# Packed attention with a gated convolution on one Trainium2 core: the low words of the float64 weights go from DVE to GpSimd, with a new plan and a new issue order

## The chip, the core and the metric

The kernel runs on one core of a Trainium2 chip. The metric is device time in microseconds. A profiled execution gives, beside its own device time, its span: the time from its first to its last instruction. The engines are named as in the profile: PE (TensorE matmul; PEld is its weight load), DVE (VectorE), ACT (ScalarE), POOL (GpSimd) and SP (SyncE, which issues the transfers).

## What is computed

Eight batches of eight heads; 576 positions of 64 values; 32 packed queries per head. Attention is done twice, first from the packed queries to the keys and values, then from the queries to the 32 packed results, and a feed-forward layer follows, in which a convolution of three taps along the sequence makes a gate:

```python
p_packed = sm_attn(p, k, v)                    # [8, 8, 32, 64]
out = sm_attn(q, p_packed, p_packed)           # [8, 8, 576, 64]
x = out.transpose(0, 2, 1, 3).reshape(8, 576, 512)
h = np.maximum(x @ w_in, 0.0)                  # 512 -> 1024
conv_out = sum(conv_w[t] * hp[:, t:t + 576, :] for t in range(3))   # hp: h with a zero at each end
gate = 1.0 / (1.0 + np.exp(-conv_out))
result = h * gate @ w_out                      # 1024 -> 512
```

q, k, v and p are float32. The three weight arrays arrive as float64: the generator multiplies them by a float64 scalar.

## The kernel before

**Groups and tiles.** Four heads of a batch make a group `g` (16 groups, two per batch). `load_kq` and `load_v` bring k, q and v. `head_transpose` turns k and q: groups 0 to 3 with PE (L444) and a copy by ACT (L450), the others with a DVE transpose (L427). `queries` (L484, L487, L493 or L495) prepares the packed queries. `attention` makes the first scores (L460, written `big<-kT,pT`), the maximum on DVE (L515), the exponential on ACT (L519), the product with v (L557), the second scores (L460, `big<-qT,ppT`), a softmax on DVE (L591 to L615) with the exponential on ACT (L601), and splits the weights into a high part (`a2hi`, ACT L619) and a rest (`a2lo`, DVE L621). `packed_weight` multiplies the packed results with half of `w_in` (L641), splits the product in `ghi` (ACT L656) and `glo` (for batches 0 and 1 PE L660 and ACT L664). `ffn1(b, j)` is twelve matmuls of 288 columns (L705) for 128 of the 1024 hidden rows, then ReLU, taps, tanh and gate on ACT and DVE (L717 to L733). `ffn2(m)` multiplies 128 rows of the gated result with `w_out` (L794, split by L744 and L747).

**The float64 weights.** `w_in` and `w_out` come in four tiles each (`load_weight`, L305), 256 rows by 512 columns of 8 bytes, as 128 partitions with 1024 pairs of 32-bit words. They land in three places in turn: `stage`, and two parts of the second gate buffer (`hgt`). `narrow` makes float32 of them in three passes: ACT scales the upper words (L275), DVE turns the low words into a number of 0 to 7 (L277), and DVE puts the two together (L282). The low and the upper pass need only the tile; the third needs both. `conv_w` goes the same way with 24 rows. A tile of `w_out` is then split into `wo_hi` and `wo_lo` with ACT and PE (L333, L338, L342).

**What sets the order.** Every function is a stream of `Step`s, one for each engine instruction or small run of them. The table `ORDER`, two characters a step, says which stream gives the next step; so each engine's queue is written out by hand, and an engine that waits holds all that is behind it. Beside that `Flow` keeps a model of time: when each step could start, with a lag between engines, buffers as tokens and the transfers. Until the first `ffn2` product is done, `Flow.fill` puts `idle` matmuls (L251, 128x128 on the identity matrix) on PE where the model sees PE waiting. The model emits nothing else: it adds no wait to the program. Steps with small stationary tiles (L460, L557, L641) are `tiled`: PE works with 64x32 or 128x32 tiles there.

Of the kernel before, what the change touches and what calls it, by code (L numbers as in the profile page):

```python
# [21 lines left out]
    "0002043m0408043u0304030305060b3l0c06013k050b060c0g0c0c0b060605053q3v3k0e06070e070a3k063v06063k0j060e3v09060j3s0k"  # L22
    "0f0j0o060k0e0f3n0k0i0h3r3r060k0d063k0e0m0d3k3r060d0r0e0e0d060e060e060m060e0m0r3t0m0m3t0s0r400e3w0w0s0e0s0n0z0e0e"
    "3t0s0l0e0n060z0z0l0l0e3y170e46460m0q060m0e0u0e0u0l0m460m0e41460p410m170m0e0m0u17480u3x493x480v410v0m0u3x48410m4a"
    "49484a10474849474a3z0m414948413z491f4a49124248470u0u4a4a474b124b0t490u124b0t14433z0u0t0m4a434b0m4c0t4d1f4b4b434c"
    "0u441f4d0x4c4b3z12120u4e18434e3z1a0u4c120m4d4c4g3o6e130u1a154c3z0u131a124c6e450m0u434e4d45126e0u4e434g4f0m456e4g"
    "1a0u1n0m0u124f6e1n451l4d4e4f6e0u454f4d1a4h1c4e4e0u0u4f4g1b0y1k4d451b4i4f4f114j4i881n884k4i6e1g4h6f4j6e6e4i6f6e4k"
    "4h4k4i4j4i89161i121a4k4j4i6e1i6f6f121e1a4j4k4l891d126f6f6f6f4j4k4l1i6f1o4k6g121s4l1i4l6g4h124l8a4m1a4l6f1a1j4m1q"
    "191j1i1a6f4m4j121i6g1q8a1w6g6h6e4n6g4m6h1q204n1a1v6g1i6g4m1v4l1h6g4m1a4n124m121r1v4n6g6g236f8b1a6g4o121i4n1i4o4p"
    "6h6h4o4p4p1a236h124o8b4o6h4n1q6g4p1a6h6h6h4p6h4o1m4o1a1y4n234p4p1q1i6h1i1q4q282b1y4r6i1r1y6i1y1a1i6i126i6i1q1a2b"  # L30
    "4r6i12241a4q4q1z6i6j1a6i1a4r1i6i6i4s6i2b1p4s6j4s1q4t4u1q4s1i1y1i4t4s264t1t4t1q1z6k1y2g6j2c4u6j1y4u4s261i6j2j4u6j"
    "4s6k6j264u2j4v4t2j1q6j271i4u1u4v226i4u6j266j4t2e1x4w2k6j4t1i4v1q2e1i1q6k4w2e4v2a1i1q6h2f2e4v3p6k6k6k4w1y1i274x26"
    "6k1q6k6l1y4x6l216k6k6k2f4x1q6k4x2m1y4v50266m1q6l6l4w264v1q26262r2m6l2h4w6l2m2r506l4x2r6j6l4y4w2e1q2n2z4y4y2z1y1y"
# [12 lines left out]
    "3i6563613i63633i656162816175747466676587747466757j7h686666676766757575676867836675767575756766686775757j696a7k7k"
    "76697i6868696969766a6a687j6a696876767676766a6a7687766b7g69787h6a7m7k8578876b6b6c7q7676756c6b6c7n6d7o777l7n6c7l7l"
    "6c6d6d6c6d77777i7b777q7m6c7n7n7p6b7m6b6d6b7x6d6d7e817n7o7p7n7n7r79797o777r7777777t7t7o7b777c7e777p7x7s7a7s7c7p7a"
    "7a7a7a7y7a7a7a7u7t7w7w7w7u7a7a7x7v7v7u7z7v7f7f7x7x7y7x7z7x7y7z7d7d7d7d7z7d7d7d7d7y8c7d7d7d7d7d7d7d7d7d8c7d"
# [3 lines left out]
class Step:  # L53
# [5 lines left out]
    def __init__(self, engine, ns, after=(), take=(), give=(), sets=None, cols=0, tiled=False, parts=1, loose=False):  # L59
        self.engine, self.ns, self.after, self.take, self.give = engine, ns, after, take, give  # L60
        self.sets, self.cols, self.tiled, self.parts, self.loose = sets, cols, tiled, parts, loose


class Flow:
# [11 lines left out]
    LAG = {  # L76
        "PE": dict(PE=0, ACT=197, DVE=196, SP=200, POOL=200),
        "ACT": dict(PE=216, ACT=153, DVE=142, SP=200, POOL=200),
        "DVE": dict(PE=256, ACT=128, DVE=127, SP=200, POOL=200),
        "DATA": dict(PE=300, ACT=300, DVE=300, SP=0, POOL=0),  # L80
    }
    ISSUE = dict(SP=(465, 1100), POOL=(1050, 1000))
    LATER, LANES = 620, 8
# [101 lines left out]
def tile_packed_attention_conv_gate(  # L185
# [15 lines left out]
    HG = 4  # L201
# [867 lines left out]
```

## Time and profile before

| | us |
|---|---|
| median of 3 runs (402.21 to 402.48) | 402.41 |
| the profiled execution | 402.01 |
| its span | 400.2 |
| PE busy in the span | 392.2 (98%) |
| DVE busy | 365.5 (91%) |
| ACT busy | 284.1 (71%) |
| POOL busy | 1.6 |

The profile's first part is the busy time of each engine, the second shows it in 40 equal slices. Its table of groups adds up instructions of one line; the timeline lists them in order of time, and writes the idle time of the engine before an instruction in brackets, with what ended it. A line `x14` in a timeline is fourteen records drawn together. A 128x128 float32 matmul of the program leaves two records on PE. PE's ends are modelled and the records overlap, so that what a matmul costs is read from the distance between starts, or between ends.

### The profile page before, as it was taken

How to read it: one execution, taken by the hardware profiler on the slowest of the kernel's cores; microseconds unless marked ns; L12 is line 12 of the kernel's file. 1: busy time of each engine (PE TensorE's matmuls, PEld its weight loads, DVE VectorE, ACT ScalarE, POOL GpSimd, SP SyncE). 2: the span in 40 equal slices, each digit the busy share in tenths (PEclk: the TensorE clock that was granted, in tenths of full speed). 3: DMA queues.
4: the chain of work that ended last, by engine and by line, in shares of the span. 5: the costliest groups of instructions: out<-in, count | busy, mean ns of one | idle time of the engine just before them, and what ended most of it. 6: DMA issues, size and time to landing. Idle time of an engine off the chain costs nothing.

```text
span 400.2 us, 8463 instructions
## 1 busy us (share of the span) xinstructions
PE 392.2 (98%) x3393; PEld 318.8 (80%) x3393; DVE 365.5 (91%) x532; ACT 284.1 (71%) x497; POOL 1.6 (0%) x16
## 2 busy tenths in 40 slices
PE   7899999999999999999999999999999999999996
PEld 6668676778868877878869687878788787889996
DVE  0789999999999999999999999999999999999751
ACT  4989999977687588666765659738657678876440
POOL 1000000000000000000000000000000000000000
PEclk9999999999999999999999999999999999999999
DMA  8999999999858782966483539113600110001202
GB/s 304 357 361 267 276 264 163 128 156 146 121 94 112 122 196 68 156 88 153 79 153 79 97 100 157 48 51 97 122 2 27 52 41 19 23 2 52 78 28 79
DMA packets 140378, 49.19 MB, mean 123 GB/s; under 512 B 121244, under 2 KB 132788, under 8 KB 140340
## 3 DMA queue, kind: packets, MB, share of 16 engines
q1 hardware_dynamic: 140340, 48.67, 55.8%
q8 instruction: 26, 0.43, 0.5%
q14 instruction: 12, 0.10, 0.1%
HBM read 37.25 MB, written 9.44 MB: 117 GB/s over the span
## 4 chain that ended last, share of the span: by engine, by line
PE 84%; ACT 8%; DMA 5%; SPq 1%; issue 1%
PE fo L794 44%; PE big L705 23%; PE big L460 3%; PE big L641 3%; DMA q<-in_q_dram 3%; PE big L926 3%; DMA v<-in_v_dram 2%; PE sm L926 2%; PE sm L557 2%; ACT hgt L731 1%; ACT hgt L721 1%; PE big L547 1%; ACT hgt L275 1%; ACT glo L664 1%; SPq L404 1%; PE sm L794 1%
## 5 line engine op out<-in xcount | busy, mean ns | idle before, releaser
L794 PE MATMUL fo<-wo_hi,xhi 128*128 128x512 f32 x240 | 97.9, 408 | 0.0
L794 PE MATMUL fo<-wo_lo,xhi 128*128 128x512 f32 x240 | 94.8, 395 | 0.0
L794 PE MATMUL fo<-wo_hi,xlo 128*128 128x512 f32 x240 | 94.5, 394 | 0.0
L717 ACT ACTIVATE hbuf<-big 128x576 f32<-128x576 f32 x64 | 42.3, 668 | 30.1 <-PE big L705 29.5
L731 ACT ACTIVATE hgt<-hgt 128x576 f32<-128x576 f32 x64 | 43.9, 696 | 18.8 <-DVE hgt L727 18.6
L794 PEld LDWEIGHTS fo<-wo_hi,xhi 128*128 128x128 f32 x240 | 45.3, 189 | 13.3 <-issue 2.5
L705 PE MATMUL big<-a2hi,ghi 128*128 128x288 f32 x256 | 55.6, 298 | 0.1
L705 PE MATMUL big<-a2hi,glo 128*128 128x288 f32 x256 | 54.5, 294 | 0.0
L705 PE MATMUL big<-a2lo,ghi 128*128 128x288 f32 x256 | 54.3, 294 | 0.0
L794 PEld LDWEIGHTS fo<-wo_lo,xhi 128*128 128x128 f32 x240 | 45.1, 188 | 11.2
L723 DVE SCALAR_TENSOR_TENSOR hgt<-hbuf,cw,hgt 128x576 f32<-128x576 f32 x64 | 51.1, 802 | 2.5 <-ACT hgt L721 2.3
L794 PEld LDWEIGHTS fo<-wo_hi,xlo 128*128 128x128 f32 x240 | 45.1, 188 | 7.9
L727 DVE SCALAR_TENSOR_TENSOR hgt<-hbuf,cw,hgt 128x576 f32<-128x576 f32 x64 | 50.7, 803 | 0.4
L721 ACT ACTIVATE hgt<-hbuf,cw 128x576 f32<-128x576 f32 x64 | 50.3, 792 | 1.0
L733 DVE SCALAR_TENSOR_TENSOR hgt<-hgt,hbuf 128x576 f32<-128x576 f32 x64 | 47.1, 745 | 0.7 <-ACT hgt L731 0.4
L705 PEld LDWEIGHTS big<-a2hi,ghi 128*128 128x128 f32 x256 | 42.7, 188 | 5.1 <-ACT glo L664 1.0
L705 PEld LDWEIGHTS big<-a2lo,ghi 128*128 128x128 f32 x256 | 40.9, 188 | 0.0
L705 PEld LDWEIGHTS big<-a2hi,glo 128*128 128x128 f32 x256 | 40.9, 188 | 0.0
L747 DVE TENSOR_TENSOR xlo<-hgt,xhi 128x1024 fp32r<-128x1024 f32 (+1 forms) x36 | 35.8, 1002 | 0.0
L858 ACT COPY o<-fo 128x512 f32<-128x512 f32 (+1 forms) x32 | 18.5, 580 | 21.2 <-PE fo L794 19.6
L744 ACT CAST xhi<-hgt 128x1024 fp32r<-128x1024 f32 (+1 forms) x36 | 31.5, 881 | 2.2 <-DVE hgt L733 2.2
L515 DVE TENSOR_REDUCE nm<-big 128x1 f32<-128x576 f32 x16 | 11.9, 746 | 11.6 <-PE big L460 11.5
(191 smaller groups left out, 604.1 us busy)
## 6 DMA issues: line engine op xcount, KB each, us to landing
out_dram<-o SPq DMA_DIRECT2D x35, 256.0 KB, 3.3
v<-in_v_dram SPq DMA_DIRECT2D x16, 512.0 KB, 5.9
k<-in_k_dram SPq DMA_DIRECT2D x48, 144.0 KB, 4.2
q<-in_q_dram SPq DMA_DIRECT2D x48, 144.0 KB, 4.1
hgt<-in_moe_w_in_dram SPq DMA_DIRECT2D x3, 1024.0 KB, 11.2
hgt<-in_moe_w_out_dram SPq DMA_DIRECT2D x3, 1024.0 KB, 6.6
a1T<-stage SPq DMA_DIRECT2D x96, 20.0 KB, 1.8
hgt<-in_k_dram SPq DMA_DIRECT2D x2, 576.0 KB, 5.1
```

Source lines behind the costliest of these rows:

```text
L705: nc.tensor.matmul(out=t[:, hf, :SH], lhsT=w[:, gg, js], rhs=x[:, hf * SH : (hf + 1) * SH], start=n == 0, stop=n == 3 * NG - 1,)
L717: nc.scalar.activation(out=h[:, 1 : S + 1].rearrange("c (f s) -> c f s", f=2), in_=t[:, :, :SH], func=AF.Relu, scale=0.5)
L721: nc.scalar.activation(out=d, in_=h[:, 1 : S + 1], func=AF.Copy, scale=cw[:, NJ + j : NJ + j + 1])
L723: nc.vector.scalar_tensor_tensor(out=d, in0=h[:, 0:S], scalar=cw[:, j : j + 1], in1=d, op0=ALU.mult, op1=ALU.add)
L727: nc.vector.scalar_tensor_tensor(out=d, in0=h[:, 2 : S + 2], scalar=cw[:, 2 * NJ + j : 2 * NJ + j + 1], in1=d, op0=ALU.mult, op1=ALU.add)
L731: nc.scalar.activation(out=d, in_=d, func=AF.Tanh)
L733: nc.vector.scalar_tensor_tensor(out=d, in0=d, scalar=1.0, in1=h[:, 1 : S + 1], op0=ALU.add, op1=ALU.mult)
L744: nc.scalar.copy(out=hi[:, js, o], in_=src[:, js])
L747: nc.vector.tensor_tensor(out=lo[:, js, o], in0=src[:, js], in1=hi[:, js, o].bitcast(F32), op=ALU.subtract)
L794: nc.tensor.matmul(out=t[:, : fs.stop - fs.start], lhsT=x, rhs=w[:, c, fs], start=c + i == 0, stop=c == NJ - 1 and i == 2)
L858: nc.scalar.copy(out=o[:, fs], in_=sums_of[m, q][:, : fs.stop - fs.start])
L926: nc.tensor.matmul(out=turns[m, bank][:, at : at + 256], lhsT=x[:, c, :], rhs=y[:, c, :], start=first and c + i == 0, stop=c == 3 and i == ...
```

## The change

The pass over the low words of the eight weight tiles (not that of `conv_w`) is issued on GpSimd in place of DVE. It keeps its operands; the third pass on DVE now waits for GpSimd as well as for ACT. In the model of time, DVE steps that are marked `cols=1` and the GpSimd pass exclude each other (`self.port`): neither starts in the model before the last such step has ended. The GpSimd pass is given 1500 ns there. The model also counts the descriptors of transfers in flight (`ring`), keeps the transfers of SP and GpSimd apart, and has other constants for issue times. `ORDER` is a new table.

```diff
-    ISSUE = dict(SP=(465, 1100), POOL=(1050, 1000))
-    LATER, LANES = 620, 8
+    ISSUE = dict(SP=(465, 1100), POOL=(900, 1000))
+    LATER, LANES = 640, 8
...
+    ROOMY, SLACK = 60000, 500
+    RING = 288
...
+        if step.engine in ("DVE", "POOL") and step.cols:
+            at = max(at, self.port)
         return max(at, self.free[step.engine] + (self.tail(step.tiled) if step.engine == "PE" else 0))
...
                 end = (at + step.ns, engine)
                 self.free[engine] = end[0]
+                if engine != "ACT" and step.cols:
+                    self.port = end[0]
...
+    BY_POOL = range(8)
+    POOL_LOW, POOL_BOTH = 1500, 2200
...
         yield Step("ACT", 93 + m * 14 // 15, after=after, sets=[("up", key)])
         nc.scalar.activation(out=up, in_=up, func=AF.Prelu, scale=F64_REBIAS, alpha=-(2.0**32))
-        yield Step("DVE", 68 + m * 100 // 192, after=after, loose=True)
-        nc.vector.tensor_scalar(
+        pool = key in BY_POOL
+        side = nc.gpsimd if pool else nc.vector
+        at = Step("POOL", POOL_LOW, after=after, loose=True, parts=0, sets=[("low", key)], cols=1)
+        yield at if pool else Step("DVE", 68 + m * 100 // 192, after=after, loose=True, cols=1)
+        side.tensor_scalar(
             out=low.bitcast(I32), in0=low.bitcast(U32), scalar1=2.0**-29, scalar2=7.0, op0=ALU.mult, op1=ALU.min
         )
-        yield Step("DVE", 69 + m * 100 // 96, after=[("up", key)], take=take, sets=sets)
+        yield Step("DVE", 69 + m * 100 // 96, after=[("up", key)] + [("low", key)] * pool, take=take, sets=sets, cols=1)
...
-    "0002043m0408043u0304030305060b3l0c06013k050b060c0g0c0c0b060605053q3v3k0e06070e070a3k063v06063k0j060e3v09060j3s0k"
+    "00040404023m0308050403030505060b0b050c0b0j06060c0c0c0j0j3u06010e0g070706063v3k06063k063q0k060e0e3v0a0k0k0k3v3k3k"
...
```

Ten DVE steps further down (softmax, `a2lo`, taps and gate, `xlo`) get `cols=1` and nothing else. In the changed file a line stands 22 lines further down than before (L444 is L466, L705 is L727), the idle matmul is L270 in place of L251, and the passes of `narrow` are L294, L299 and L304.

The queues show what moved. The first place is PE from the transposes of q of group 2 (`big<-ident,q`) to the first `ffn1` product (`big<-a2hi,ghi`). Before:

```order
L251 MATMUL idle<-ident 128x128 x3
L444 MATMUL big<-ident,q 128x128 x5
L487 MATMUL sm<-ident,pm 128x128
L444 MATMUL big<-ident,q 128x128 x4
L641 MATMUL big<-w_in_sb,ppT 32x512 x8
L557 MATMUL sm<-v,a1T 32x64 x20
L460 MATMUL big<-kT,pT 32x288 x8
L581 MATMUL sm<-ident,pb 128x128
L660 MATMUL big<-ghi,minus 128x512 x2
L460 MATMUL big<-qT,ppT 32x288 x8
L487 MATMUL sm<-ident,pm 128x128
L251 MATMUL idle<-ident 128x128 x7
```

And the same stretch after the change:

```order
L270 MATMUL idle<-ident 128x128
L466 MATMUL big<-ident,q 128x128 x9
L663 MATMUL big<-w_in_sb,ppT 32x512 x8
L579 MATMUL sm<-v,a1T 32x64 x20
L482 MATMUL big<-kT,pT 32x288 x8
L603 MATMUL sm<-ident,pb 128x128
L682 MATMUL big<-ghi,minus 128x512 x2
L270 MATMUL idle<-ident 128x128 x2
L482 MATMUL big<-qT,ppT 32x288 x8
L727 MATMUL big<-a2hi,ghi 128x288 x2
```

The two transposes of packed queries (L487) have gone elsewhere, and seven idle matmuls ahead of the first product have become none, with two ahead of the last scores.

The second is ACT's queue at the same place, up to `glo`, which the first product needs. Before:

```order
L450 COPY qT<-big 128x640
L484 ACTIVATE pm<-p 128x128
L656 CAST ghi<-big 128x1024
L576 ACTIVATE pb<-sm,rs 128x128
L450 COPY qT<-big 128x512
L584 COPY ppT<-sm 128x128
L619 CAST a2hi<-a2t 128x576
L275 ACTIVATE stage<-stage 128x1024
L664 CAST glo<-big 128x1024
```

After:

```order
L472 COPY qT<-big 128x640
L472 COPY qT<-big 128x512
L678 CAST ghi<-big 128x1024
L598 ACTIVATE pb<-sm,rs 128x128
L641 CAST a2hi<-a2t 128x576
L606 COPY ppT<-sm 128x128
L686 CAST glo<-big 128x1024
L294 ACTIVATE stage<-stage 128x1024
```

The upper pass over the fourth tile (`stage`) has gone from ahead of `glo` to behind it.

DVE's queue up to the `a2lo` of group 1, which the first product needs too. Before:

```order
L282 SCALAR_TENSOR_TENSOR w_in_sb<-hgt_77 128x2x512
L604 TENSOR_REDUCE sm_460<-s_425 128x18
L629 RECIPROCAL rs<-rs 128x1
L606 TENSOR_SCALAR sm_460<-sm_460 128x18
L608 RECIPROCAL sm_460<-sm_460 128x18
L621 TENSOR_TENSOR a2lo<-a2t,a2hi 128x576
L610 TENSOR_TENSOR s_425<-s_425,sm_460 128x576
L615 STREAM_TRANSPOSE a2t<-s_425 128x576
L515 TENSOR_REDUCE nm<-big 128x1
L277 TENSOR_SCALAR stage<-stage 128x1024
L591 STREAM_TRANSPOSE s_559<-big 128x576
L621 TENSOR_TENSOR a2lo<-a2t,a2hi 128x576
```

After:

```order
L304 SCALAR_TENSOR_TENSOR w_in_sb<-hgt_77 128x2x512
L626 TENSOR_REDUCE sm_458<-s_404 128x18
L628 TENSOR_SCALAR sm_458<-sm_458 128x18
L630 RECIPROCAL sm_458<-sm_458 128x18
L632 TENSOR_TENSOR s_404<-s_404,sm_458 128x576
L637 STREAM_TRANSPOSE a2t<-s_404 128x576
L537 TENSOR_REDUCE nm<-big 128x1
L643 TENSOR_TENSOR a2lo<-a2t,a2hi 128x576
```

The low pass of `stage` is gone from DVE, and the transpose of group 2's scores now stands behind `a2lo`.

The third place is SP's queue around the q of group 2 (`q<-in_q_dram`). Before:

```order
L305 DMA hgt_77<-in_moe_w_in_dram 128x2x1024
L404 DMA k<-in_k_dram 128x1152
L477 DMA p<-in_p_dram 128x4x64
L404 DMA q<-in_q_dram 128x1152
L388 DMA v<-in_v_dram 128x4x256
```

After:

```order
L327 DMA hgt_77<-in_moe_w_in_dram 128x2x1024
L426 DMA k<-in_k_dram 128x1152
L426 DMA q<-in_q_dram 128x1152
L410 DMA v<-in_v_dram 128x4x256
L414 DMA v<-in_v_dram 64x4x64
```

The second load of packed queries no longer stands ahead of q; it comes four transfers later, and q of group 3 is now issued ahead of the four transfers of k of group 4.

## Rows read from the trace of the kernel before

**Rows 1.** The page: busy time, and the granted clock in 40 slices.
```profile
PE 392.2 (98%) x3393; PEld 318.8 (80%) x3393; DVE 365.5 (91%) x532; ACT 284.1 (71%) x497; POOL 1.6 (0%) x16
...
PEclk9999999999999999999999999999999999999999
```

**Rows 2.** PE's waits: who waited, for whom, us in total, times, longest.
```profile
PE big L444 <- DMA hgt<-in_q_dram: 1.5, 1, 1.5
PE big L444 <- DMA q<-in_q_dram: 0.5, 1, 0.5
...
PE big L444 <- ACT glo L664: 0.2, 1, 0.2
```

**Rows 3.** Windows: length, busy PE PEld DVE ACT POOL, PEclk, DMA share, GB/s.
```profile
20.00:28.00 8.00, 7.57 (x112) 5.48 (x112) 6.87 (x13) 6.12 (x16) 0.00 (x0) 1.00 1.06 358
...
35.00:75.00 40.00, 39.68 (x368) 28.80 (x367) 39.66 (x62) 39.56 (x67) 0.24 (x2) 1.00 1.05 221
```

**Rows 4.** The idle matmuls: durations in ns, first and last start.
```profile
L251 PE MATMUL idle<-ident x70: 271/275/579, 1.7 to 48.3; 128*128 128x128 f32 x70
```

**Rows 5.** PE's timeline, q of group 2 to the first product: start, us, instruction.
```profile
28.18 0.74 PE L444 MATMUL big<-ident,q 128*128 128x128 f32 x5 [0.54 <-DMA q<-in_q_dram]
...
32.64 0.71 PE L460 MATMUL big<-qT,ppT 64*32 64x288 f32 x16
...
33.45 1.73 PE L251 MATMUL idle<-ident 128*128 128x128 f32 x14
34.93 0.51 PE L705 MATMUL big<-a2hi,ghi 128*128 128x288 f32 x2
```

**Rows 6.** ACT's timeline ahead of the first product.
```profile
32.45 0.68 ACT L619 CAST a2hi<-a2t 128x576 fp32r<-128x576 f32 x1
33.03 1.17 ACT L275 ACTIVATE stage<-stage 128x1024 f32<-128x1024 f32 x1
34.07 1.02 ACT L664 CAST glo<-big 128x1024 fp32r<-128x1024 f32 x1
```

**Rows 7.** DVE's timeline ahead of the first product, and at one later low pass.
```profile
32.61 0.69 DVE L277 TENSOR_SCALAR stage<-stage 128x1024 int32<-128x1024 uint32 x1
...
34.17 0.71 DVE L621 TENSOR_TENSOR a2lo<-a2t,a2hi 128x576 fp32r<-128x576 f32 x1
...
63.92 0.69 DVE L277 TENSOR_SCALAR hgt<-hgt 128x1024 int32<-128x1024 uint32 x1
64.53 0.17 DVE L606 TENSOR_SCALAR sm<-sm 128x18 f32<-128x18 f32 x1
```

**Rows 8.** Three groups of POOL: busy us, mean ns of one, idle before.
```profile
L246 POOL MEMSET v<- 64x256 f32 x2 | 0.6, 306 | 0.0
masks.py:199 POOL TENSOR_SCALAR_AFFINE_SELECT ident<-ident 128x128 f32<-128x128 f32 x1 | 0.3, 287 | 0.0
...
masks.py:197 POOL MEMSET ident<- 128x128 f32 x1 | 0.2, 205 | 0.3 <-POOLq L1054 0.3
```

**Rows 9.** Timeline: the first `xlo` and the product that uses it.
```profile
61.27 0.68 DVE L747 TENSOR_TENSOR xlo<-hgt,xhi 128x512 fp32r<-128x512 f32 x1
...
63.54 0.48 PE L794 MATMUL fo<-wo_hi,xhi 128*128 128x512 f32 x1
```

**Rows 10.** PE's timeline around three tiled steps in a row.
```profile
80.28 0.63 PE L660 MATMUL big<-ghi,minus 128*128 128x512 f32 x2
80.84 0.72 PE L460 MATMUL big<-kT,pT 64*32 64x288 f32 x16
81.35 0.69 PE L460 MATMUL big<-qT,ppT 64*32 64x288 f32 x16
81.97 0.77 PE L557 MATMUL sm<-v,a1T 128*32 128x64 f32 x40
82.67 0.50 PE L794 MATMUL fo<-wo_hi,xhi 128*128 128x512 f32 x1
83.01 0.39 PE L794 MATMUL fo<-wo_hi,xlo 128*128 128x512 f32 x1
```

More of the change, by code (lines that the diff above doesn't have):

```diff
@@ L50, with __init__ @@
+    "7b7a7z7a7a777u7w7y7c7a7x7s7s7v7v7a7x7z7a7x7v7y7y7a7e7x7y7a7d7d7d7d7a7d7d7d7z7z7a7d8c8c7d7d7d7d7d7d7d7d7d7d"
 )
 class Step:
-    def __init__(self, engine, ns, after=(), take=(), give=(), sets=None, cols=0, tiled=False, parts=1, loose=False):
+    def __init__(self, engine, ns, after=(), take=(), give=(), sets=None, cols=0, tiled=False, parts=1, loose=False, ring=8):
         self.engine, self.ns, self.after, self.take, self.give = engine, ns, after, take, give
-        self.sets, self.cols, self.tiled, self.parts, self.loose = sets, cols, tiled, parts, loose
+        self.sets, self.cols, self.tiled, self.parts, self.loose, self.ring = sets, cols, tiled, parts, loose, ring
@@ L90, in __init__ @@
         self.free = dict(PE=2500.0, ACT=1900.0, DVE=600.0, SP=580.0, POOL=1350.0)
-        self.data = 2700.0
+        self.data = dict(SP=2700.0, POOL=2700.0)
         self.issued = 0
         self.flights = [0.0] * 7
+        self.queued = []
+        self.port = 0.0
         self.windows = {}
@@ L147, in transfers @@
                 at = max(at, self.flights.pop(0))
+                while self.queued and (self.queued[0][0] <= at or sum(n for _, n in self.queued) + step.ring > self.RING):
+                    at = max(at, self.queued.pop(0)[0])
             at += self.LATER if step.engine == "SP" and self.issued >= self.LANES else issue
             self.issued += step.engine == "SP"
-            slow = next((x for t, x in self.SLOW if self.data < t), 1.0)
-            self.data = max(self.data, at + delay) + step.ns / step.parts * slow
+            slow = next((x for t, x in self.SLOW if self.data["SP"] < t), 1.0)
+            ns = step.ns / step.parts * slow
+            start = max(self.data[step.engine], at + delay)
             if step.engine == "SP":
-                self.flights.append(self.data)
-        return at, self.data
+                landed = self.data["SP"] = start + ns
+                self.flights.append(landed)
+                self.queued.append((landed, step.ring))
+            else:
+                landed = self.data["POOL"] = start + min(max(0.0, self.data["SP"] - start), ns) + ns
+                self.data["SP"] = max(self.data["SP"], start) + ns
+        return at, landed + (self.SLACK if at > self.ROOMY else 0.0)
     def run(self, order):
@@ L169, in run @@
                 self.tiled = step.tiled
-            elif step.engine in self.ISSUE:
+            elif step.engine in self.ISSUE and step.parts:
                 self.free[engine], t = self.transfers(step, at)
@@ L301, in load_weight @@
         _, _, src, st = weight_tile(i)
-        yield Step("SP", 2500, after=[("wp", i - 3)] if i >= 3 else [], sets=[("wd", i)])
+        yield Step("SP", 2500, after=[("wp", i - 3)] if i >= 3 else [], sets=[("wd", i)], ring=16)
         if src.dtype != F32:
@@ L384, in load_v @@
         b, gg = divmod(g, NG)
-        yield Step("SP", 2250, take=["v"], sets=[("v", g)], parts=2)
+        yield Step("SP", 2250, take=["v"], sets=[("v", g)], parts=2, ring=24)
         t = grp[g]["v"] = vfree.pop(0)
@@ L725, in ffn1 @@
         )
[L726 removed]
+        yield Step("DVE", 729, cols=1)
         nc.vector.scalar_tensor_tensor(
@@ L744, in convert @@
             nc.scalar.copy(out=hi[:, js, o], in_=src[:, js])
-        yield Step("DVE", 68 + (js.stop - js.start) * 128 * 100 // 96, sets=spans)
+        yield Step("DVE", 68 + (js.stop - js.start) * 128 * 100 // 96, sets=spans, cols=1)
         for src, o in cuts:
@@ L850, in load_block @@
             nc.scalar.copy(out=hi[:, :, o], in_=src[:, js])
-        yield Step("DVE", 601, sets=[("x", m, k)])
+        yield Step("DVE", 601, sets=[("x", m, k)], cols=1)
         for src, o in cuts_of(m):
```

69 lines of the change are left out of this document (34 added, 35 removed).

## The prediction

> **What bounds the kernel now.** First the busy times: PE is busy for 392.2 us of a span of 400.2, DVE for 365.5, ACT for 284.1, and POOL for 1.6 [rows 1]. So PE sets the end, and the question is where its time is not work. Next PE's waits: the largest behind the start are for two transfers of q, 1.5 and 0.5 us, and the smallest is 0.2 for `glo` [rows 2]; all belong to the first groups and batches. The windows say the same: from 35 to 75 us PE is busy for 39.68 of 40 us, and so are DVE (39.66) and ACT (39.56) [rows 3]. The list of waits has no entry for a later stage. There is one more kind of lost time that is not called idle: the idle matmuls, 70 records, 35 instructions, all between 1.7 and 48.3 us [rows 4]. Fourteen records stand between 33.45 and 34.93 us [rows 5], so one costs 1.48 / 14 = 0.106 us and all of them 7.4 us.
>
> A gain can therefore come only from three places on PE: fewer idle matmuls, shorter waits in the first 50 us, and cheaper changes between tiled and plain matmuls. All other matmuls are the same before and after the change, in number and in shape.
>
> **The change part by part.** *DVE loses eight passes.* One lasts 0.69 us, and the next instruction starts 0.61 us after it (63.92 to 64.53) [rows 7]: 8 x 0.61 = 4.9 us less for DVE. That is not yet a gain, since DVE is not what ends last.
>
> *GpSimd gets eight passes.* No row shows one. Two memsets bound it from below: 205 ns for 128 elements a partition and 306 for 256 [rows 8], so 0.8 ns an element and 0.1 us fixed, 0.9 us for 1024. From above, the select on 128 elements, 287 ns [rows 8], taken eight times: 2.3 us. I take the select, which reads and computes as the new pass does, with the fixed 0.1 us counted once: 1.47 ns an element, 1.6 us. On the path I cost it at nothing: a pass needs only its tile, GpSimd has nothing else to do then, and the third pass also waits for ACT's pass over the upper words, 1.17 us [rows 6], which stands in a busy queue. If that cover is gone, as for the first tile that lands, 1.6 - 1.17 = 0.4 us (at most 1.1) are late on a DVE that still has gaps.
>
> *The third pass gets a wait.* Behind it in DVE's queue stand the softmax of a group and its `a2lo`; PE waits for these. With GpSimd starting at the landing, the wait ends before ACT's.
>
> *Two engines at one port.* The changed plan holds apart the GpSimd pass and DVE steps with two operands in SBUF. It emits no wait for it; if the chip lets only one of them run, DVE stands still for what is left of a pass. The trace of before has no such pair. The bounds are 0 and 8 x 1.6 = 12.8 us of DVE's time; below zero there is nothing, as neither engine gets faster by the other's work. Ahead of the first product about half of DVE's instructions read two SBUF operands, so I take half of a pass, 6.4 us. Against the 4.9 saved DVE is then 1.5 us later by 64 us. The first `xlo` ends at 61.27 + 0.68 = 61.95 and is used at 63.54 [rows 9]: 1.6 us of cover, which this just fills. Cost on PE: 0.
>
> *The order up to the first `ffn1` product.* In before it starts at 34.93 us [rows 5], behind three things, and all three move.
> - PE. q of group 2 was released by its transfer at 28.18. The 128 KB of packed queries ahead of it go away: 0.128 MB at 358 GB/s [rows 3] is 0.36 us, so 27.8. From there to the last scores it took 32.64 - 28.18 = 4.46 us [rows 5]; less one plain transpose of packed queries (0.1), plus four idle records (0.4): 4.8. With 0.65 for the scores themselves [rows 10] the queue can reach the product at 27.8 + 4.8 + 0.65 = 33.3.
> - ACT. `glo` started at 34.07, behind `stage`'s upper pass, which held ACT from 33.03 to 34.07 [rows 6]. That pass is now behind it, and the chain starts 0.36 earlier: `glo` is written near 33.7. The product started 0.16 before the end of `glo`'s record (34.07 + 1.02 = 35.09), so here near 33.5.
> - DVE. `a2lo` started at 34.17, behind a low pass at 32.61 and a transpose of scores; its `a2hi` had ended at 32.45 + 0.68 = 33.13 [rows 6, 7]. With both out of the way it starts when `a2hi` is there, near 32.8, and ends near 33.5.
> The last of the three gives 33.5: 34.9 - 33.5 = 1.4 us earlier. The 1.5 us that went into fourteen idle records are gone with it; they are the same gain and are not counted twice.
>
> *Behind it.* The idle matmuls there were four, and are eight: 4 x 2 x 0.106 = 0.85 us lost, if the waits that they fill are real. What stays of the gain is 1.4 - 0.85 = 0.55.
>
> *Tiled runs.* Scores directly behind other scores end 0.48 us after them, behind plain matmuls 0.65 (80.28 + 0.63 = 80.91, then 81.56, then 82.04); the first plain product behind tiled work ends 0.43 us after it, the next 0.23 [rows 10]. So entering costs 0.16 and leaving 0.20. The 63 tiled steps stand in 30 runs before and 28 after. Counted through both queues, two products with `w_in` save an entry, one score loses one, and two exits are saved: -0.32 + 0.16 - 0.40 = -0.55 us, the most of it behind 75 us where nothing hides it.
>
> *Moved transfers and the rest.* q of group 3 goes ahead of the four transfers of k of group 4: 0.576 MB, some 1.6 us later at 358 GB/s. DVE's transpose of that k has moved by more, behind six gate instructions in place of one, so nothing. The load of packed queries that comes later feeds group 4, which is not needed ahead of 33 us. The model's new constants emit nothing but idle matmuls, which are counted.
>
> *Sum.* 0.55 + 0.55 = 1.1 us. A second way of counting goes through PE's whole queue and leaves the waits as they are: 4 idle instructions less, 0.85, and the runs, 0.55: 1.4. I take the middle, 1.25 us. The profiled execution lasted 402.01 us and would last 400.8; the median of the runs is 0.4 above it, 402.41, and gives 401.2.
>
> **The rivals.** *The gain is given back.* ACT gets nothing off its queue, and has 0.4 us to spare in the 40 us behind the first product [rows 3]. An earlier product only makes PE wait for ACT's copies and ReLUs there; what is left is the tiled runs, partly: 402.1 (401.6 to 403.2). For it: three engines are full at once. Against it: ACT's own pass in front of `glo` is what moved, so ACT's later work moves with PE's.
>
> *The port.* Here the two engines exclude each other on the chip, and a pass meets a two-operand instruction nearly always. In the stretch behind 39 us DVE's queue is mostly gate instructions, and each has two operands in SBUF. Six of eight passes cost DVE their whole 1.6 us: 9.6 - 4.9 = 4.7 us late. Less the cover of 1.6, PE loses 3.1 and keeps the 1.25: 402.4 + 1.9 = 404.3. It decides from a loss of some 1 us a pass (8 x 1 = 4.9 + 1.6 + 1.25, about), or from passes of over 2 us. For it: nothing in the program keeps the two apart, only the order. The Trainium skill has this as a rule (SBUF — State Buffer, "Who interferes with whom"): the port pair that GpSimd shares with DVE is a lock that the first one holds for its whole instruction, also against a DVE instruction with two SBUF inputs if GpSimd reads SBUF. By that rule this rival's mechanism is real and only the meetings are open; no row of before shows it. Against it: the new order has one-operand instructions at several of the landings.
>
> *The clock.* The granted clock is full in all slices [rows 1]. Ahead of the first product there are 23 idle instructions in place of 31, and PE's wait for q of group 1 has fewer of them in front. If the clock falls to 1.2 GHz for a stretch of 4 us there, some 3 us of matmuls last 3 us more, less what the next transfer hides: 404. Against it: the wait is no longer than before.
>
> *The passes stay a cost without a benefit*, that is, DVE's relief is real but PE never waited for DVE: this is the case in the first rival, with the same time.
>
> **How the numbers follow.** The forecast, 399.9 to 401.6, has 0.54: the unknown terms are the waits behind the first product (-0.85 to +0.5) and the DVE cover. A larger gain, below 399.9, has 0.04: it needs PE's waits in 35 to 75 us to go as well. The gain given back, 0.20. The port, 0.16, and the clock, 0.06. A measurement of this kernel can tell some 0.2% from no change, 0.8 us, that is 401.6 to 403.2. Faster: 0.54 + 0.04 = 0.58. Same: 0.20. Slower: 0.22. The range from 399.9 to 403.6 holds the forecast, the gain given back and the mild end of the port, 0.8 in all.
>
> **What would show it.** In the profile of after: 62 records of idle matmuls; the first `ffn1` product at 33.5 us and q of group 2 released at 27.8; `glo` ahead of the upper pass on ACT; GpSimd passes of 0.9 to 2.3 us. For the port: DVE instructions with two operands that last longer than 0.7 to 0.8 us, or idle time in front of them, while GpSimd is busy. The prediction is wrong if the first product is early and PE then waits for ACT or DVE between 35 and 75 us, if DVE's gate instructions are stretched, or if the clock shows less than 9 in a slice behind the first.

## The result and the profile after

| | before | after |
|---|---|---|
| median, us | 402.45 (402.21 to 403.31) | 405.87 (405.35 to 406.36) |
| profiled execution, us | 402.01 | 405.85 |
| its span, us | 400.2 | 404.1 |
| last matmul ends, us | 397.10 | 399.94 |

The changed kernel is slower: the ratio of the times is 1.0080, with a 95% interval from 1.0062 to 1.0098, some 3.2 us. The forecast was 401.2, in a range up to 403.6. Medians here and below are of fast executions alone: one of 571.58 us (e4, whose median with it is 402.58) and one of 767.73 (e10) are left out. Line numbers after are 22 higher than before; for the idle matmuls and the passes over the weights 19 to 22.

The page first, as in [rows 1]: busy time, and the granted clock in 40 slices.

```profile
PE 393.5 (97%) x3385; PEld 319.2 (79%) x3385; DVE 365.2 (90%) x524; ACT 284.0 (70%) x497; POOL 34.2 (8%) x24
PEclk9999999999999999999999999999999999999999
```

Two things stand there. The clock was full throughout. And GpSimd was busy for 34.2 us in place of 1.6: eight passes, so about 4 us each, where the forecast took 1.6 and bounded it at 2.3. DVE has eight instructions fewer and is only 0.3 us less busy.

Six of the eight passes in GpSimd's timeline (start, duration, instruction, and in brackets the idle time in front with what ended it):

```profile
10.90 3.82 POOL L299 TENSOR_SCALAR stage<-stage 128x1024 int32<-128x1024 uint32 x1 [8.95 <-DMA stage<-in_moe_w_in_dram]
24.56 4.09 POOL L299 TENSOR_SCALAR hgt<-hgt 128x1024 int32<-128x1024 uint32 x1 [3.57 <-DMA hgt<-in_moe_w_in_dram]
32.27 3.79 POOL L299 TENSOR_SCALAR stage<-stage 128x1024 int32<-128x1024 uint32 x1 [3.62 <-DMA stage<-in_moe_w_out_dram]
36.14 3.86 POOL L299 TENSOR_SCALAR hgt<-hgt 128x1024 int32<-128x1024 uint32 x1
43.81 3.99 POOL L299 TENSOR_SCALAR hgt<-hgt 128x1024 int32<-128x1024 uint32 x1 [3.81 <-DMA hgt<-in_moe_w_out_dram]
49.16 4.72 POOL L299 TENSOR_SCALAR hgt<-hgt 128x1024 int32<-128x1024 uint32 x1 [1.36 <-DVE hgt L749]
```

And the third passes in DVE's timeline, the first, third, fourth and fifth of eight:

```profile
14.76 1.23 DVE L304 SCALAR_TENSOR_TENSOR w_in_sb<-stage 128x1024 int32<-128x1024 int32 x1 [1.02 <-POOL stage L299]
28.69 1.23 DVE L304 SCALAR_TENSOR_TENSOR w_in_sb<-hgt 128x1024 int32<-128x1024 int32 x1 [1.39 <-POOL hgt L299]
36.34 2.02 DVE L304 SCALAR_TENSOR_TENSOR tmp<-stage 128x1024 int32<-128x1024 int32 x1
40.03 1.25 DVE L304 SCALAR_TENSOR_TENSOR w_in_sb<-hgt 128x1024 int32<-128x1024 int32 x1 [1.68 <-ACT hgt L743]
```

DVE waits 1.02, 1.39 and 1.68 us in front of three of them, 4.1 us in all. The third wait is put down to ACT, but the pass over that tile ran from 36.14 to 40.00 and DVE went on at 40.03: it was GpSimd again. That pass also started late, because the pass of 32.27 held GpSimd until 36.06. The instruction at 36.34 shows the other thing: it met the start of a GpSimd pass at 36.14 and lasted 2.02 us, where others of its line last 1.18 to 1.25.

On PE, where [rows 2] had 0.2 us of waiting for ACT in all, there is now a list. These are PE's waits for ACT of 0.4 us and more (us in total, times, longest):

```profile
PE big L727 <- ACT a L541: 0.7, 1, 0.7
PE big L727 <- ACT glo L686: 0.5, 2, 0.3
PE sm L603 <- ACT pb L598: 0.4, 1, 0.4
PE big L482 <- ACT hbuf L739: 0.4, 1, 0.4
```

They stand in this part of PE's timeline. The first row is the products with `w_in`, the second the first `ffn1` product, whose start was forecast:

```profile
28.85 2.19 PE L663 MATMUL big<-w_in_sb,ppT 64*32 64x512 f32 x16
34.54 0.52 PE L727 MATMUL big<-a2hi,ghi 128*128 128x288 f32 x2 [0.20 <-ACT glo L686]
49.18 0.72 PE L482 MATMUL big<-kT,pT 64*32 64x288 f32 x16 [0.36 <-ACT hbuf L739]
53.10 0.33 PE L603 MATMUL sm<-ident,pb 128*128 128x128 f32 x1 [0.44 <-ACT pb L598]
54.16 0.53 PE L727 MATMUL big<-a2hi,ghi 128*128 128x288 f32 x2 [0.73 <-ACT a L541]
```

The sixteen products with `w_in` (L663) took 2.19 us. They need the tile whose third pass ended at 28.69 + 1.23 = 29.92, after a GpSimd pass that ended at 28.65. The waiting is inside the row, between its eighth and ninth matmul, and the list of PE's waits doesn't name it. Only the rows of this line alone do: PE's weight load sat idle for 1.0 us until DVE's third pass (L304). Behind 57 us PE waits for nothing, as before. The delay has been collected by then and is carried to the end.

### The profile page after: what moved, and what is told of

Same layout as the page of the kernel before. It is cut to its first block, busy times and chain, and to the rows that moved or that the text cites. A ratio compares the mean times of both kernels' runs of the same rounds, so it can differ in the third digit from the quotient of the medians.

```text
span 404.1 us, 8464 instructions
## 1 busy us (share of the span) xinstructions
PE 393.5 (97%) x3385; PEld 319.2 (79%) x3385; DVE 365.2 (90%) x524; ACT 284.0 (70%) x497; POOL 34.2 (8%) x24
## 4 chain that ended last, share of the span: by engine, by line
PE 86%; DMA 5%; DVE 3%; ACT 3%; POOL 1%; SPq 1%; issue 0%; DVEq 0%; ACTq 0%
PE fo L816 44%; PE big L727 23%; PE big L482 3%; PE big L663 3%; DMA hgt<-in_moe_w_in_dram 3%; PE big L948 3%; DMA v<-in_v_dram 2%; PE sm L948 2%; PE sm L579 2%; PE big L360 2%; POOL hgt L299 1%; PE big L569 1%; PE sm L816 1%; DVE w_in_sb L304 1%; DVE hgt L755 1%; ACT hgt L294 1%
## 5 line engine op out<-in xcount | busy, mean ns | idle before, releaser
L816 PE MATMUL fo<-wo_hi,xhi 128*128 128x512 f32 (+1 forms) x244 | 98.9, 405 | 0.0
L816 PE MATMUL fo<-wo_lo,xhi 128*128 128x512 f32 (+1 forms) x244 | 95.9, 393 | 0.0
L816 PE MATMUL fo<-wo_hi,xlo 128*128 128x512 f32 (+1 forms) x244 | 95.7, 392 | 0.0
L816 PEld LDWEIGHTS fo<-wo_hi,xhi 128*128 128x128 f32 x244 | 46.0, 189 | 14.7 <-issue 2.2
L727 PE MATMUL big<-a2hi,ghi 128*128 128x288 f32 x256 | 55.5, 298 | 1.2 <-ACT a L541 0.7
L745 DVE SCALAR_TENSOR_TENSOR hgt<-hbuf,cw,hgt 128x576 f32<-128x576 f32 x64 | 52.1, 820 | 3.2 <-ACT hgt L743 3.0
L816 PEld LDWEIGHTS fo<-wo_lo,xhi 128*128 128x128 f32 x244 | 45.8, 188 | 11.1
L727 PE MATMUL big<-a2hi,glo 128*128 128x288 f32 x256 | 54.4, 294 | 0.0
L727 PE MATMUL big<-a2lo,ghi 128*128 128x288 f32 x256 | 54.2, 293 | 0.0
L816 PEld LDWEIGHTS fo<-wo_hi,xlo 128*128 128x128 f32 x244 | 45.9, 188 | 8.2
L749 DVE SCALAR_TENSOR_TENSOR hgt<-hbuf,cw,hgt 128x576 f32<-128x576 f32 x64 | 51.8, 820 | 0.5
L743 ACT ACTIVATE hgt<-hbuf,cw 128x576 f32<-128x576 f32 x64 | 49.2, 778 | 0.9
L727 PEld LDWEIGHTS big<-a2hi,ghi 128*128 128x128 f32 x256 | 42.5, 188 | 7.3 <-ACT glo L686 1.6
L727 PEld LDWEIGHTS big<-a2lo,ghi 128*128 128x128 f32 x256 | 40.9, 188 | 0.0
L727 PEld LDWEIGHTS big<-a2hi,glo 128*128 128x128 f32 x256 | 40.9, 188 | 0.0
L299 POOL TENSOR_SCALAR hgt<-hgt 128x1024 int32<-128x1024 uint32 x6 | 25.0, 4160 | 19.5 <-DMA hgt<-in_moe_w_out_dram 12.1
```

What stands on the lines that cost most here:

```text
L299: side.tensor_scalar(out=low.bitcast(I32), in0=low.bitcast(U32), scalar1=2.0**-29, scalar2=7.0, op0=ALU.mult, op1=ALU.min)
L727: nc.tensor.matmul(out=t[:, hf, :SH], lhsT=w[:, gg, js], rhs=x[:, hf * SH : (hf + 1) * SH], start=n == 0, stop=n == 3 * NG - 1,)
L743: nc.scalar.activation(out=d, in_=h[:, 1 : S + 1], func=AF.Copy, scale=cw[:, NJ + j : NJ + j + 1])
L745: nc.vector.scalar_tensor_tensor(out=d, in0=h[:, 0:S], scalar=cw[:, j : j + 1], in1=d, op0=ALU.mult, op1=ALU.add)
L749: nc.vector.scalar_tensor_tensor(out=d, in0=h[:, 2 : S + 2], scalar=cw[:, 2 * NJ + j : 2 * NJ + j + 1], in1=d, op0=ALU.mult, op1=ALU.add)
L816: nc.tensor.matmul(out=t[:, : fs.stop - fs.start], lhsT=x, rhs=w[:, c, fs], start=c + i == 0, stop=c == NJ - 1 and i == 2)
```

## The experiments

Three causes were held against each other: the **length** of GpSimd's pass (the third pass waits for it), the **port** (DVE's instructions with two operands in SBUF are held up while GpSimd works), and the **order** (the new issue order is worse, whichever engine makes the passes). All ratios are to the kernel before, timed on the same chip; 0.001 is 0.4 us.

| run | what it is | median us | ratio, 95% interval |
|---|---|---|---|
| after | the changed kernel | 405.87 | 1.0080 (1.0062 to 1.0098) |
| e1 | new order, passes on DVE | 401.36 | 0.9970 (0.9955 to 0.9986) |
| e2 | old order, passes on GpSimd | 405.90 | 1.0077 (1.0050 to 1.0104) |
| e2z | e2, third pass doesn't wait | 403.01 | 1.0007 (0.9993 to 1.0021) |
| e8 | after, third pass doesn't wait | 402.06 | 1.0000 (0.9978 to 1.0021) |
| e4b | after, pass over one pair | 401.76 | 0.9974 (0.9962 to 0.9987) |
| e4 | after, pass over half of the pairs | 402.27 | 0.9998 (0.9980 to 1.0017) |
| e5 | after, pass of one operation | 403.83 | 1.0024 (1.0010 to 1.0039) |
| e3 | after, only `w_out` on GpSimd | 405.28 | 1.0074 (1.0048 to 1.0100) |
| e10 | after, one store cut in eight | 405.09 | 1.0063 (1.0040 to 1.0086) |
| e8s | e8, one store cut in eight | 401.17 | 0.9966 (0.9946 to 0.9987) |
| e4bs | e4b, one store cut in eight | 400.89 | 0.9955 (0.9939 to 0.9972) |

### The engine against the order: e1 and e2

```diff
-        side = nc.gpsimd if pool else nc.vector      # e1, in the changed kernel
+        side = nc.vector
...
-        nc.vector.tensor_scalar(                     # e2, in the kernel before
+        side = nc.gpsimd if key in range(8) else nc.vector
+        side.tensor_scalar(
```

> The changed kernel with its order, its plan and its 31 idle instructions, only that all eight low passes run on DVE again, at the places where the plan lets them start. The three causes that stand against each other: the length of a GpSimd pass (3.8 to 4.7 us in the profile of after, so that DVE's third pass waits for it, 1.0 us at 14.8, 1.4 at 28.7, 1.7 at 40.0); the port (DVE instructions with two operands in SBUF lasted 0.8 to 0.9 us longer where a pass begins, some 3.7 us over the kernel); the new order itself, whichever engine makes the pass. By length or port the loss goes with GpSimd's passes: 401.2 to 403.0, near or under the kernel before, with DVE 4.9 us busier. By the order the time stays at 405 or more, since DVE then has its eight passes on top.

> The kernel before, with its order, its plan and its 35 idle instructions, only that the eight low passes run on GpSimd. By length or port it becomes slower by about what the changed kernel lost, 404.5 to 408: the third passes stand at 14.6, 18.9, 27.4, 36.1 and 38.0 us there, each 2 to 4 us behind the landing of its tile, so those with under 3.8 us wait. By the order alone it gains what DVE is relieved of, or nothing: 401 to 402.6.

e1 is 1.2 us faster than the kernel before, and e2 is 3.1 us slower. So the order isn't the cause: the loss comes and goes with the engine that makes the pass, under either order. e1 is also a version that beats both kernels.

The same two places in e1's trace, PE's products with `w_in` and first `ffn1` product:

```profile
29.14 1.09 PE L663 MATMUL big<-w_in_sb,ppT 64*32 64x512 f32 x16
33.65 0.53 PE L727 MATMUL big<-a2hi,ghi 128*128 128x288 f32 x2
```

and three of DVE's third passes, which now wait for nothing:

```profile
27.81 1.23 DVE L304 SCALAR_TENSOR_TENSOR w_in_sb<-hgt 128x1024 int32<-128x1024 int32 x1
37.38 1.22 DVE L304 SCALAR_TENSOR_TENSOR w_in_sb<-hgt 128x1024 int32<-128x1024 int32 x1
46.33 1.22 DVE L304 SCALAR_TENSOR_TENSOR tmp<-hgt 128x1024 int32<-128x1024 int32 x1
```

The sixteen products take 1.09 us in place of 2.19, and the first `ffn1` product starts at 33.65: the forecast had said 33.5.

Since e1 and after issue the same matmuls in the same order, the delay can be read place by place, as the start of one instruction in both timelines (us):

| place | e1 | after | later |
|---|---|---|---|
| first `ffn1` product (L727) | 33.65 | 34.54 | 0.9 |
| first scores from keys behind 47 us (L482) | 47.62 | 49.18 | 1.6 |
| transpose of packed results (L603) | 50.55 | 53.10 | 2.6 |
| first `ffn2` product (L816) | 65.07 | 68.17 | 3.1 |
| end of the last matmul | 396.74 | 399.94 | 3.2 |

### The wait against the port: e8 and e2z

```diff
+        if pool:
+            low = hbuf[0][:, 0:1].broadcast_to([128, m])   # a column of zeros
...
         nc.vector.scalar_tensor_tensor(
             out=out,
...
```

> The changed kernel, with GpSimd's passes as they are, but the third pass of these eight tiles takes a column of zeros in place of the low words, so it doesn't wait for GpSimd any more (left out: the three lowest bits of the weights). What is left of GpSimd's passes is their use of the port. If their length is the cause, the waits in front of the third pass fall to under 0.3 us and the time to 401.5 to 403.0, although the two-operand instructions on DVE are still stretched by 0.8 us. If it is the port, the stretched instructions and the time stay, 404.5 to 406. If it is the order, both are wrong and the time stays too.

> The order of the kernel before, the eight passes on GpSimd, and zeros in place of the low words for the third pass, so that it doesn't wait (left out: the three lowest bits of the weights). With the wait this order took 405.9. If the waits for a pass of 3.8 us are the cause there too, it falls to 402 to 402.6, the time of the kernel before; if the port is, it stays above 404.5.

GpSimd's passes are all there, as long as before (3.8 to 4.2 us in e8), and the loss is gone: from 1.0080 to 1.0000 under the new order, from 1.0077 to 1.0007 under the old. That is the wait, 3.2 and 2.8 us. In e2's trace six third passes wait for GpSimd, 6.0 us in all, and in the traces of e8 and e2z none does. (e2z's median is 0.4 us over its expected range; the kernel before, timed beside it, was 0.3 over its usual 402.4.) The instruction that met the start of a pass was still stretched, as the fourth third pass of e8 shows:

```profile
36.66 2.04 DVE L309 SCALAR_TENSOR_TENSOR tmp<-stage,hbuf 128x1024 int32<-128x1024 int32 x1
```

So the port is real, but by the medians it isn't what the kernel lost by. It isn't free in every execution. The profiled ones lasted 404.74 us (e8) and 403.48 (e8s, the same with one store cut, see below), where the medians are 402.06 and 401.17. In that of e8s no third pass waits for GpSimd and the clock is full, and yet the last matmul ends at 398.58, 2.4 us later than in its partner with a pass of 0.2 us (e4bs, 396.13). DVE's rows are stretched by some 5 us in sum there, and two of the stretched ones stand in front of the places where PE is late in after, too:

```profile
24.97 1.70 DVE L648 TENSOR_TENSOR a2lo<-a2t,a2hi 128x576 fp32r<-128x576 f32 x1
48.62 2.35 DVE L760 SCALAR_TENSOR_TENSOR hgt<-hgt,hbuf 128x576 f32<-128x576 f32 x2
```

In e4bs the first lasts 0.75 us. In e8s the first tile also landed 1.2 us later (12.05 us, in e4bs 10.88), so not all of the 2.4 need be the port's. What sets such an execution apart from the median one no run shows.

### How long may the pass be: e4b, e4 and e5

```diff
+        part = low[:, : 1] if pool else low           # e4b; in e4: low[:, : m // 2]
...
-            out=low.bitcast(I32), in0=low.bitcast(U32), scalar1=2.0**-29, scalar2=7.0, op0=ALU.mult, op1=ALU.min
+            out=part.bitcast(I32), in0=part.bitcast(U32), scalar1=2.0**-29, scalar2=7.0, op0=ALU.mult, op1=ALU.min
...
+            side.tensor_scalar(out=low.bitcast(I32), in0=low.bitcast(U32), scalar1=2.0**-29, scalar2=None, op0=ALU.mult)   # e5, all pairs
```

> The changed kernel, with a low pass on GpSimd over one pair a partition in place of 1024, whose result the third pass reads for all weights (left out: the low words of all other pairs). So the wait's place, the engine and the order stay, and the pass is some 0.1 to 0.3 us long. By length or port 401.0 to 402.5, the time that was forecast for a pass that costs nothing on the path; what lies between this run and the one with zeros for low words is the price of the port alone. By the order it stays at 405 to 406.

> The changed kernel with GpSimd's pass over 512 pairs a partition in place of 1024; the third pass takes each low word for two weights (left out: the low words of the other half of the pairs). The pass should last half of 3.8 us, 1.9, which is inside the bounds that the prediction set for it (0.9 to 2.3). If the mis-sized pass is all that was wrong, the waits in front of the third pass are gone at this length and the time is 401.2 to 402.3. If the loss grows in proportion to the pass, whatever it covers, half of it stays, 403.4 to 404.

> The changed kernel with a GpSimd pass of one operation, the multiplication, without the minimum (changed: the largest low words give 8 in place of 7). In the measurement alone that pass lasted 2.85 us in place of 3.72. A point between the pass of 2.0 us (402.6) and that of 3.8 (405.9). By the length theory each third pass that waited 1.0 to 1.7 us waits 0.9 less: 403 to 404.2.

| pass, us (most of the eight) | DVE's waits for it, sum, us | ratio |
|---|---|---|
| 0.2 (e4b) | 0 | 0.9974 |
| 2.0 (e4) | 1.1 | 0.9998 |
| 3.0 (e5) | 2.5 | 1.0024 |
| 3.9 (after) | 4.1 | 1.0080 |

The time follows the pass. e4's time, 402.27, lies at the upper edge of what was expected, but the waits, expected to be gone, are not: 0.31 and 0.78 us remain. By the ratios it is 1.0 us slower than e4b, just clear of the noise; in the traces its last matmul ends 0.5 us later (396.71 and 396.22). So a pass of 2.0 us is cheap, but not shown to be free. The third pass of the second `w_out` tile still waits, and so does that of e5. The rows of GpSimd and DVE for this tile, first e4, then e5:

```profile
44.68 2.01 POOL L300 TENSOR_SCALAR hgt<-hgt 128x512 int32<-128x512 uint32 x1 [7.36 <-DMA hgt<-in_moe_w_out_dram]
46.73 1.23 DVE L309 SCALAR_TENSOR_TENSOR tmp<-hgt 128x1024 int32<-128x1024 int32 x1 [0.78 <-POOL hgt L300]
```

```profile
43.79 3.31 POOL L300 TENSOR_SCALAR hgt<-hgt 128x1024 int32<-128x1024 uint32 x1 [5.74 <-DMA hgt<-in_moe_w_out_dram]
47.14 1.23 DVE L307 SCALAR_TENSOR_TENSOR tmp<-hgt 128x1024 int32<-128x1024 int32 x1 [0.86 <-POOL hgt L300]
```

GpSimd starts as the tile lands, at 44.68 and 43.79; DVE's queue is there at 46.73 - 0.78 = 45.95 and 47.14 - 0.86 = 46.28. So there are 1.3 and 2.5 us for the pass, and what it takes beyond that is a wait.

### Which tiles: e3

```diff
-        side = nc.gpsimd if pool else nc.vector
+        side = nc.gpsimd if pool and key >= 4 else nc.vector
```

> The changed kernel, with only the four w_out tiles left to GpSimd; the four w_in tiles have their low pass on DVE. All three waits for GpSimd that the profile of after shows stand at w_in tiles, and the four longest stretches of DVE instructions with two operands in SBUF (36.3, 43.3, 50.2 and 62.8 us) at the w_out tiles. If the wait for a long pass is the cause, the time falls to 401.2 to 402.6. If the port is, it keeps most of the loss: 404 to 405.5.

405.28: by the number the port was right, but the trace shows a wait as well. The expectation of the length theory had looked only at the waits that after shows. Without those at the `w_in` tiles, DVE's queue comes earlier to the second `w_out` tile, and a wait stands there that after had hidden behind the earlier ones. DVE's timeline in e3:

```profile
48.05 1.23 DVE L304 SCALAR_TENSOR_TENSOR tmp<-hgt 128x1024 int32<-128x1024 int32 x1 [1.77 <-POOL hgt L299]
49.20 2.35 DVE L755 SCALAR_TENSOR_TENSOR hgt<-hgt,hbuf 128x576 f32<-128x576 f32 x2
51.54 0.73 DVE L537 TENSOR_REDUCE nm<-big 128x1 f32<-128x576 f32 x1
```

Behind the wait of 1.77 us come two gate instructions, stretched from 1.43 (e1) to 2.35 by the start of the next pass, and behind them the maximum that ACT's exponential needs, for which PE waits. Up to there PE is within 0.6 us of e1; the transpose of packed results starts 1.6 us later (52.13), the first `ffn2` product 2.1 (67.19). Wait and stretch together are 2.7 us here, so this run alone doesn't separate the two causes; e8 does by its median, since all stretches and no waits are in it. Another 0.8 us of e3's distance to e1 comes behind the last matmul (3.94 us to the end, in place of 3.17; see e10).

### The pass and the port by themselves: m1

No diff: a program of its own, which does nothing of the computation.

> No part of the computation: a measurement of the pass and of the port alone. GpSimd makes the pass in several forms (as it is; multiplication only; int32 to int32; float32 to float32; contiguous; in halves), beside a row of DVE instructions with two operands in SBUF, with one, and with one of two in PSUM, and with DVE idle. By the length theory the pass lasts 3.8 us alone too, so it isn't contention that makes it long. By the port theory DVE's instructions with two operands in SBUF stop for the whole pass, 3.8 us, or their sum grows by at least that; by what the profile of after shows only one of them, the one that the pass's start meets, grows by 0.8 to 1.2 us. Those with one operand, or with one in PSUM, keep their time.

GpSimd's pass alone, with DVE idle: as it is, with multiplication only, and over contiguous words.

```profile
84.50 3.72 POOL L53 TENSOR_SCALAR words<-words 128x1024 int32<-128x1024 uint32 x1
88.98 2.85 POOL L53 TENSOR_SCALAR words<-words 128x1024 int32<-128x1024 uint32 x1
101.55 3.63 POOL L53 TENSOR_SCALAR flat<-flat 128x1024 int32<-128x1024 uint32 x1
```

Now DVE's row: two operands in SBUF beside one pass, without a pass; then one operand, in the same two ways; then one of two operands in PSUM, beside a pass (ns: least, median, most).

```profile
L58 DVE TENSOR_TENSOR z<-x,y x10: 748/758/1517, 10.3 to 18.2; 128x576 f32<-128x576 f32 x10
L58 DVE TENSOR_TENSOR z<-x,y x4: 748/758/759, 7.0 to 9.4; 128x576 f32<-128x576 f32 x4
L61 DVE TENSOR_SCALAR z<-x x10: 450/460/1221, 30.0 to 36.0; 128x576 f32<-128x576 f32 x10
L61 DVE TENSOR_SCALAR z<-x x4: 449/460/461, 27.9 to 29.4; 128x576 f32<-128x576 f32 x4
L64 DVE TENSOR_TENSOR z<-bank,y x10: 680/691/691, 46.1 to 52.6; 128x512 f32<-128x512 f32 x10
```

The length theory holds: 3.72 us with nothing beside it. The second operation costs 0.87 of it, the stride of two words 0.09; int32 or float32 in place of uint32 changed nothing. The port theory holds in part. One of the ten instructions with two operands grew by 0.76 us, to 1.52; the others keep their 0.76 although the pass goes on. It is not the one that runs as the pass begins at 11.23 us (11.12 to 11.88) but the next, from 11.91; and the pass is longer beside it, 4.27 us. Against the expectation the instructions with one operand in SBUF are held up too, two of ten, by 0.76 each. The one with an operand in PSUM is not.

### The last microsecond: e10, e8s and e4bs

```diff
-        nc.sync.dma_start(out=...[m * 128 : (m + 1) * 128, fs], in_=o[:, fs])
+        r = 16 if m == 27 else 128
+        for h in range(0, 128, r):
+            nc.sync.dma_start(out=...[m * 128 + h : m * 128 + h + r, fs], in_=o[h : h + r, fs])
```

> The changed kernel, with the store of one earlier block of 128 output rows cut into eight of 16 rows, which only makes SyncE's program seven issues longer. In the trace of after one packet of 8 KB of queue 14, the queue of instructions, lies at 401.45 us, between the issue and the landing of the last stored half block, and from the last matmul to the end it takes 4.13 us; in the kernel before, and with the passes on DVE, the packet comes after the landing and it takes 3.13 and 3.17. If that fetch belongs to SyncE's program and delays the landing, its place moves and the time falls by 1.0 us, to 404.9. If the last microsecond has another cause, the time stays at 405.9.

> Zeros in place of the low words, so that no third pass waits for GpSimd, and the earlier store cut into eight, so that the fetch of code is out of the last landing. What is left of GpSimd's passes is the port: beside a pass of 3.8 us one DVE instruction in the measurement alone grew by 0.76 us, 8 x 0.76 = 6.1 us of DVE's time for the 4.9 that it was relieved of. If PE's end follows DVE there, this run is 0.5 to 1.2 us above its partner with the short pass; if the cover takes it, both agree within 0.4. Without the 0.9 of the fetch: 400.9 to 401.6.

> The partner: GpSimd's pass over one pair a partition, with the same store cut into eight. No wait, no port, no fetch in the last landing: the new order with DVE relieved of eight passes. 400.6 to 401.2, 0.9 under the same kernel without the cut store (401.76); the difference to the new order with the passes on DVE (401.36) is then all that the relief of DVE is worth, 0.2 to 0.7 us.

The last two stores, of half a block each, in the list of transfers (count, KB, median us from issue to landing): first after, then e1, then e10.

```profile
out_dram<-o SPq DMA_DIRECT2D x2, 128.0 KB, 2.7
```

```profile
out_dram<-o SPq DMA_DIRECT2D x2, 128.0 KB, 1.7
```

```profile
out_dram<-o SPq DMA_DIRECT2D x8, 32.0 KB, 1.7
out_dram<-o SPq DMA_DIRECT2D x2, 128.0 KB, 1.7
```

With the longer program on SyncE the packet of the instruction queue moves from 401.45 to 397.82 us, the landing takes 1.7 us again, and the time from the last matmul to the end falls from 4.13 to 3.10 us. In the medians it is 0.7 us (1.0080 to 1.0063), in the pair e4b and e4bs 0.8. The intervals overlap; the microsecond itself is in the traces. It isn't peculiar to after: in six of the thirteen traces (after, e3, e4, e4b, e5, e8) the packet lies between the issue and the landing of the last store, and from the last matmul to the end it takes 3.75 to 4.13 us; in the seven others it doesn't, and it takes 3.10 to 3.17. The table of passes above has it in all four rows.

e8s and e4bs differ by the port alone: 0.9966 and 0.9955, 0.4 us, which the intervals don't tell from nothing. The same pair without the cut store, e8 and e4b, gives 1.0 us (1.0000 and 0.9974), at the edge of the noise. e4bs and e1 differ by DVE's eight passes: 0.9955 and 0.9970, 0.6 us, not told apart either.

## Why the prediction was wrong, point by point

What the changed kernel lost and gained, from the ratios, at 402.4 us: new order -1.2 (e1); relief of DVE -0.6 (e4bs less e1); port +0.4 (e8s less e4bs); waits for the long pass +3.9 (e10 less e8s); fetch of code +0.7 (after less e10). The sum, +3.2, is the measured loss by construction; the three small terms, relief, port and fetch, are inside their uncertainty, and only the waits and the new order are clear of it.

- **GpSimd gets eight passes**: this step failed. The pass lasted 3.8 to 4.7 us, not 1.6, and lies outside the bounds of 0.9 to 2.3. The upper bound was no bound: the select in [rows 8] takes 2.2 ns an element and was the nearest row, but nothing made it the dearer operation. The pass in use takes 3.6 ns an element. No row of the kernel before could have shown that.
- **The cost on the path, put at nothing**: failed with it, by 3.9 us. The cover was taken as ACT's upper pass of 1.17 us. What counts is the time from the landing of a tile to the place where DVE's queue reaches its third pass, and that is 28.69 - 1.39 - 24.56 = 2.7 us for the third tile and 1.3 to 2.5 for the second of `w_out`. Even at 2.0 us, inside the bounds, the waits remained in part, and e4 is at 0.9998 where e1 is at 0.9970; but 0.6 of these 1.1 us are the late landing (3.75 us from the last matmul to the end, in place of 3.17), and the last matmul ends as early as in e1 (396.71 and 396.74). So the size of the pass is the larger mistake, the cover the smaller.
- **The third pass gets a wait; behind it the softmax and `a2lo`, for which PE waits**: the path was right, only its wait was taken to end ahead of ACT's. At 53 us it is the maximum (L537) behind the third pass and two gate instructions.
- **Two engines at one port**: the size came out as forecast by luck: 0.76 us a pass (m1) in place of 0.8, but as a fifth of a pass of 3.7, not half of one of 1.6. 8 x 0.76 = 6.1 us against the 4.9 saved leaves DVE 1.2 later, which the forecast left to the cover. In the medians little or nothing of it reaches PE (0.4 us, or 1.0 from the other pair); in the profiled execution of e8s it may have been up to 2.4.
- **The order up to the first `ffn1` product**: right. q of group 2 is released at 27.74 in after (forecast 27.8), `glo` starts at 33.47, ahead of the upper pass (34.37). With the passes on DVE the product starts at 33.65 (forecast 33.5); in after the products with `w_in` hold it to 34.54.
- **Idle matmuls** are 62 records, as forecast. They and the **tiled runs** were not tested one by one. Their sum with the earlier product, -1.25, agrees with e1's -1.2 (interval -1.8 to -0.6).
- **The rivals.** The port, 404.3, had named passes of over 2 us as a point from which it decides: such passes came, but the loss came through the wait. The clock was full in after. It fell in the profiled execution of e8: from 21.4 to 24.8 us the granted clock is 0.51, the level of 1.2 GHz, after 1.4 us with PE busy for 0.77. It left little behind: e8's last matmul ends 0.2 us after that of e8s, where the clock is full (398.82 and 398.58). The order's gain wasn't given back: e1 keeps it.
- **The last landing** was in no term. The kernel before has a packet of the same queue at 401.23 us, behind its last landing; in after it lies ahead of it.

## What to carry to other kernels

Before a step goes to another engine, take its time there for this very operation, or leave the upper end of the range open; a row of another operation is no bound. Compare it, tile by tile, with the time between the landing and the place where the consumer's queue arrives, and don't stop at the waits that a trace shows: once these are gone, the next tile's wait appears. A long row on PE that merges many matmuls can hold a wait that the list of PE's waits doesn't name; the rows of that line alone do.

## What the runs showed of the hardware

GpSimd takes 3.72 us for a two-operation `tensor_scalar` over 1024 elements a partition, 2.85 for one operation, against 0.69 on DVE [rows 7]. Beside one such pass one DVE instruction with two operands in SBUF grew by 0.76 us, beside two passes two (1.5 us in all), and beside two passes over 512 elements two, by 0.31 and 0.48. Of instructions with one operand in SBUF two grew within one pass, by 0.76 each; with one operand in PSUM none did.

The Trainium skill (SBUF — State Buffer, "Who interferes with whom") says that a DVE instruction with two SBUF inputs contends with a GpSimd instruction that reads SBUF, and that whoever issues first gets the shared port pair for the whole instruction. The measurement agrees that they contend, but differs on how long: beside a pass of 4.27 us DVE lost 0.76, and the next two instructions with two operands ran inside the same pass at their usual 0.76 each. What GpSimd does at the port in the rest of the pass the traces don't say.

When an 8 KB packet of the instruction queue fell between the issue and the landing of the last store, the time from the last matmul to the end was 0.6 to 1.0 us longer (six traces against seven), and seven more issues on SyncE moved the packet.
